# Attention feeding a Mish-gated MLP on one core: one attention output product moved ahead of the second group of exponentials, the MM2 portions dealt anew, and MM1's fourth block put in the second score tile

## The chip, the cores and the metric

The kernel runs on one core of one Trainium2 chip. Five engines work from queues of their own: TensorE (PE in the profile, with PEld for its weight loads), VectorE (DVE), ScalarE (ACT), GpSimd (POOL) and SyncE (SP, which here only issues DMAs). They wait for one another through semaphores. The metric is the device time of one execution in microseconds; the median of the runs is compared.

## What is computed

```python
# q, k, v: (8, 12, 448, 64); w_in: (768, 2048); w_out: (2048, 768)
scores = scale * np.matmul(q, k.transpose(0, 1, 3, 2))
m = np.max(scores, axis=-1, keepdims=True)
e = np.exp(scores - m)
attn = e / (np.sum(e, axis=-1, keepdims=True) + np.exp(-m) + 1e-09)
x = np.matmul(attn, v)                     # then heads side by side: (3584, 768)
h = x @ w_in
sp = np.where(h > 20.0, h, np.log1p(np.exp(np.minimum(h, 20.0))))
out = (h * np.tanh(sp)) @ w_out            # (3584, 768)
```

## The kernel before

Heads are worked in pairs: 8 batches of 6 pairs, 48 pairs in all, and three pairs make a unit, so there are 16 units of attention, two to a batch. The first units fill the machine. From unit 6 to unit 15, ten units, every unit has the same form, and the change is about these; the code calls them `grouped`.

**A unit's attention half** has twelve steps (`n`, 0 to 11). A step n is one score product on PE into one of three PSUM tiles sc0, sc1, sc2 (two banks each, 84, 85 and 86 in the built program's names), then the maximum of it on DVE (L369), then the exponentials on ACT (L387). Steps 0 to 8 fill both banks of a tile and take two exponentials; steps 9, 10 and 11 fill one bank and take one. Step n uses tile n mod 3, so the score of step n+3 may not start before the exponentials of step n have read their tile. I write score n, maximum n and exponentials n. In program order scores 0, 1 and 2 come at the very end of the unit before. Scores 3 and 4 are issued together after exponentials 1, scores 5 and 6 after exponentials 3, scores 7 and 8 after exponentials 5 (so that two products run at once on the halves of the PE array, L356 and L359), and scores 9, 10 and 11 one by one (L350).

**Between the steps** PE gets a filler: MM2, the second MLP product of an earlier group of rows (L616), in chunks of one matmul. A unit has three portions of 16 chunks with 384 columns and one portion of 16 chunks with 192 columns. A portion gathers in one of two further PSUM banks, mo0 and mo1 (87 and 88), and DVE copies it out (L601). The list `weight_paired` says how many chunks go in after which step, counted so that a wide chunk weighs 1, a narrow one a half, and a unit 56.

**The attention output** of a pair (`av_pair`, L497) is 8 matmuls, attention weights times v, for the three pairs of the unit before. Its operand eT is the normalised exponentials (DVE, L454), turned by a DMA that SP issues (L462) in the MM1 half of the unit before. All three products stand at step 8, behind the last filler: two in the free second banks of sc0 and sc1, copied by DVE (L517), the third in an mo bank, copied by ACT (L513) after exponentials 10. Score 11 follows them on PE.

**A unit's MLP half** is MM1: eight blocks of six matmuls of 448 columns (L556), each followed by Mish on ACT (L572) into `gT`. Exp and Mish lie in different activation tables, so ACT loads a table at both borders. Blocks 0 and 1 take the two mo banks, block 2 takes bank 0 of sc0, and blocks 3 to 7 take the mo banks in turn as Mish frees them. On DVE the MM1 half holds the denominators and the 21 normalisations.

The order on each engine is written out by hand: an engine runs its instructions in the order in which the loop makes them. Copies out of PSUM are put in a list `late`, which `flush_late` empties.

Of the kernel before, what the change touches and what calls it, by code (L numbers as in the profile page):

```python
# [15 lines left out]
UNIT_PAIRS = 3  # L16
# [3 lines left out]
def kernel(  # L20
# [17 lines left out]
    HP = H // 2  # L38
# [3 lines left out]
    UNITS_PER_B = HP // UNIT_PAIRS  # L42
    N_UNITS = B * UNITS_PER_B
    HU = 2 * UNIT_PAIRS
    FF_U = FF_T // UNITS_PER_B
# [7 lines left out]
    def pool(name, bufs, space=None):  # L53
# [16 lines left out]
    sc_tiles = [  # L70
        psum.tile([128, 2, 512], FP32, tag=f"sc{i}", name=f"sc{i}") for i in range(3)
    ]
# [43 lines left out]
    late, held, slow = deque(), deque(), deque()  # L116
    stores, defer = deque(), [False]

    def flush_late():
        while late:  # L120
            late.popleft()()
# [5 lines left out]
    def mo_take():  # L127

        if not mo_free:
            flush_late()  # L130
        return mo_free.popleft()
# [353 lines left out]
    def av_pair(p, half=None, hold=False, act=False):  # L485
        b, hp = p // HP, p % HP
        eT = att[p]["eT"]
        v_bf = casted[p]["v"]
        if b not in xT:
            xT[b] = xT_pool.tile([128, DM_T, S], BF16, tag="xT", name="xT")  # L490
        if half is not None:
            mms = av_beside.setdefault(last_step(half), [])
        av = mo_take() if half is None else free_half(half)
        for j in range(NT):
            for h in range(2):
                e_h = eT[0:SP_, j, h * S : (h + 1) * S]
                mm = nc.tensor.matmul(  # L497
                    av[h * 64 : (h + 1) * 64, 0:S],
                    lhsT=v_bf[:, h, j * D : (j + 1) * D],
                    rhs=e_h,  # L500
                    start=(j == 0), stop=(j == NT - 1),
                )
                if half is not None:
                    apart(mm, half_max[half])
                    mms.append(mm)

        def evac():
            to = xT[b][:, hp, :]
            if p == HP:
                apart(nc.scalar.copy(to, av[:, 0:S]), half_max[half])  # L510
                return
            if act:
                nc.scalar.copy(to, av[:, 0:S])  # L513
                mo_free.append(av)
                return
            if divided(p):
                read = nc.vector.tensor_copy(out=to, in_=av[:, 0:S])  # L517
            else:
                read = nc.vector.tensor_tensor(
                    out=to, in0=av[:, 0:S], in1=rb.pop(p), op=ALU.mult  # L520
                )
            if half in half_exp:
                apart(read, half_exp[half])
            elif half is not None:
                av_read[last_step(half)] = read
            if half is None:
                mo_free.append(av)

        if p in spread_copy:
            late.append(spread_copy.pop(p))  # L530
        (held if hold else slow if act or p == HP else late).append(evac)
        del att[p], casted[p], qkT[p]


# [1 line left out]

    def mm1_begin(b, ff, upto):

        bank = mm1_bank(ff)
        begun[b, ff] = (bank, upto)  # L540
        mm1(b, ff, bank, 0, upto)

# [4 lines left out]
            mm1(b, ff, bank, lo, DM_T)  # L547
            begun[b, ff] = (bank, DM_T)

    def mm1_bank(ff, ahead=2):  # L550
        at = ff % FF_U - 2
        return sc_tiles[0][:, at, :] if 0 <= at < ahead else mo_take()

    def mm1(b, ff, bank, lo, hi):
        for dm in range(lo, hi):
# [6 lines left out]

    def mm1_mish(b, ff):
        flush_late()
        at = ff % FF_U - 2
        spare = 0 <= at < (2 if b == 0 else 1)
        if (b, ff) in begun:
            h_ps, lo = begun.pop((b, ff))
        else:
            h_ps, lo = mm1_bank(ff, 2 if b == 0 else 1), 0  # L570
        mm1(b, ff, h_ps, lo, DM_T)
        nc.scalar.activation(out=gT[:, ff, b % 2 * S : b % 2 * S + S], in_=h_ps[:, 0:S], func=AF.Mish)  # L572
        if not spare:
            mo_free.append(h_ps)

    def store_rows(g, i, o_sb, cols, queue=None):
# [75 lines left out]

    weight = [5.2] + [1.0] * (steps - STEPS) + [0.4] * (STEPS - 1)
    PAIRED_FROM = first_mm2 + 2
    GROUP_AT, AV_AT_STEP = (1, 3, 5), 8
    Q_AT = (0, 6, 7)
    weight_paired = [21, 0, 12, 0, 12, 0, 5, 6, 0, 0, 0, 0]

    LEAD = UNIT_PAIRS + 1
    LOAD_AT = (0, 3, 6)  # L660
# [2 lines left out]
    BY_DMA_FROM = 2 * HP + 2 * UNIT_PAIRS  # L663
# [60 lines left out]
    for u in range(UNITS_PER_B, N_UNITS + 2 * UNITS_PER_B):  # L724
# [5 lines left out]
        p0 = u * UNIT_PAIRS  # L730
        grouped = attn and u >= PAIRED_FROM
# [7 lines left out]
        for n in range(steps):  # L739
            defer[0] = attn and u > first_mm2 and nxt < N_PAIRS  # L740
            pi, s = divmod(n, STEPS)
            p, idx = p0 + pi, p0 * STEPS + n
            late_tp = u == UNITS_PER_B and n == STEPS
            exps(idx)
            if u == UNITS_PER_B + 1 and n == 0:
                for j in range(2):
# [13 lines left out]
            while done < want:  # L760
                fn, w = filler.popleft()
                fn()
                done += w
            if grouped and n == AV_AT_STEP:
                for i in range(UNIT_PAIRS - 1):
                    av_pair(p0 + i - UNIT_PAIRS, half=p0 + i)
                flush_late()
                av_pair(p0 - 1, act=True)
            if not grouped or n + 1 not in GROUP_AT:
                scores_ahead(end)  # L770
            if n in LOAD_AT and u <= first_mm2:
                at = p0 + LOAD_AT.index(n)
# [23 lines left out]
            if (u, n) in MORE_LOADS:  # L796
                at = MORE_LOADS[u, n]
# [38 lines left out]
        b, w = (u - UNITS_PER_B) // UNITS_PER_B, u % UNITS_PER_B  # L836
# [3 lines left out]
        for f in range(FF_U):  # L840
# [22 lines left out]
            if f in (3, third) and p0 >= LATE_DIV:  # L863
                p = todo[1 + f // 5]
# [33 lines left out]
```

## Time and profile before

| what | value |
|---|---|
| median of 3 runs | 457.14 us (456.62 to 458.46) |
| the profiled execution, its own time | 459.73 us |
| its span, first to last instruction | 457.9 us |
| granted TensorE clock, mean over the span | 0.992 |
| grouped units 6 to 15 | 145.8 to 393.6 us of the span |
| instructions in the span | 8637 |

The page's first part gives each engine's busy time and the share of the span. A timeline row gives the start, the length, engine, line and operation, what is written and read, a count, and in brackets how long the engine stood idle and who released it. Matmuls overlap, so the length of one is longer than the distance from its start to the next one's start; rates are read from starts.

### The profile page before, as it was taken

Reading aid. Unit: us, or ns where it says so; the run is one execution under the profiler, and the core shown is the slowest. Engines: PE = TensorE matmul, PEld = TensorE weight load, DVE = VectorE, ACT = ScalarE, POOL = GpSimd, SP = SyncE. Lnnn points to the kernel's source line nnn. Section 1 sums busy time; section 2 is a strip of 40 time slices with the busy share of each in tenths; the row PEclk is TensorE's granted clock in tenths of the full one; section 3 lists DMA queues with packets and bytes.
Section 4 is the critical chain, followed back from the end, with each engine's and each line's share of the span. In section 5 each row is a group of like instructions: output and inputs, shape, how many; then the busy total and the mean of one; then the engine's idle time right before and its main releaser. Section 6 shows DMA issues by size and latency. Waiting matters only on the chain.

```text
span 457.9 us, 8637 instructions
## 1 busy us (share of the span) xinstructions
PE 436.2 (95%) x2991; PEld 232.1 (51%) x2991; DVE 327.3 (71%) x666; ACT 335.8 (73%) x884; POOL 138.6 (30%) x269
## 2 busy tenths in 40 slices
PE   7878699999999999999999999999999999999996
PEld 3334355445555545545454545554554555556565
DVE  5999678888797868778787878786878878311021
ACT  5999578989787969798887979796979788221300
POOL 4442638316054233232424242413233210100000
PEclk9999899999999999999999999999999999999999
DMA  8999999999999999999999999999999793920213
GB/s 233 260 209 162 246 227 212 264 235 207 242 238 273 237 279 241 250 230 283 236 257 236 259 253 229 266 214 273 229 245 252 205 243 106 246 65 2 69 36 103
DMA packets 232652, 97.93 MB, mean 214 GB/s; under 512 B 189344, under 2 KB 229152, under 8 KB 232608
## 3 DMA queue, kind: packets, MB, share of 16 engines
q1 hardware_dynamic: 225088, 91.07, 86.9%
q0 software_dynamic: 7488, 6.29, 9.3%
q8 instruction: 23, 0.38, 0.4%
q14 instruction: 21, 0.17, 0.1%
q10 hardware_dynamic: 32, 0.01, 0.0%
HBM read 45.61 MB, written 11.01 MB: 124 GB/s over the span
## 4 chain that ended last, share of the span: by engine, by line
PE 72%; ACT 10%; DVE 6%; issue 6%; DMA 3%; POOL 2%; DVEq 0%; ACTq 0%; POOLq 0%
PE mo L556 27%; PE mo L616 24%; ACT en L387 7%; PE sc L497 5%; PE sc L356 4%; PE sc L556 4%; DVE negm L369 4%; DMA eT<-en 3%; PE sc L350 2%; PE mo L497 2%; ACT L387 2%; POOL w_in_sb L177 1%; DVE o_sb L601 1%; PE sc L309 1%; DVE eT L477 1%
## 5 line engine op out<-in xcount | busy, mean ns | idle before, releaser
L387 ACT ACTIVATE en<-sc,negm 128x448 bf16<-128x448 f32 x336 | 208.9, 640 | 12.4 <-DVE negm L369 11.7
L369 DVE TENSOR_REDUCE negm<-sc 128x2 f32<-128x896 f32 x192 | 179.4, 970 | 48.5 <-PE sc L359 36.1
L616 PE MATMUL mo<-w_out_sb,gT 128*128 128x384 bf16 (+1 forms) x1040 | 159.1, 304 | 0.0
L556 PE MATMUL mo<-xT,w_in_sb 128*128 128x448 bf16 x660 | 131.7, 353 | 0.9 <-DVE xT L517 0.3
L616 PEld LDWEIGHTS <-gT 128*128 128x128 bf16 x1040 | 93.9, 98 | 60.8 <-issue 13.9
L556 PEld LDWEIGHTS <-w_in_sb 128*128 128x128 bf16 x768 | 74.3, 98 | 70.9 <-issue 5.1
L572 ACT ACTIVATE gT<-mo 128x448 bf16<-128x448 f32 x110 | 58.3, 544 | 67.9 <-PE mo L556 67.7
L387 ACT ACTIVATION_READ_ACCUMULATOR en<-sc,negm 128x1 f32 x336 | 71.0, 211 | 0.0
L454 DVE TENSOR_SCALAR en<-en,rden 128x448 bf16<-128x448 bf16 x280 | 70.6, 331 | 0.6
L601 DVE COPY o_sb<-mo 128x192 f32<-128x192 f32 (+1 forms) x65 | 32.4, 498 | 50.2 <-PE mo L616 49.0
L273 POOL TENSOR_SCALAR qd<-qT_all 64x448 bf16<-64x448 bf16 x60 | 33.6, 560 | 89.2 <-DMA qT_all<-q_cast 49.3
L356 PE MATMUL sc<-kT_all,qd 64*128 64x448 bf16 x132 | 42.0, 363 | 2.7 <-ACT en L387 1.3
L359 PE MATMUL sc<-kT_all,qd 64*128 64x448 bf16 x132 | 42.5, 367 | 0.0
L782 POOL COPY marks<-en 1x2 bf16<-1x2 bf16 x12 | 2.1, 174 | 105.6 <-DVE en L454 105.6
L194 POOL CAST q_cast<-q_f 112x512 bf16<-112x512 f32 x47 | 28.9, 614 | 5.8 <-DMA q_f<-in_q_dram 5.8
L497 PEld LDWEIGHTS <-v_bf 112*64 112x64 bf16 x384 | 19.8, 110 | 20.8 <-issue 10.4
L497 PE MATMUL sc<-eT,v_bf 112*64 112x448 bf16 x256 | 29.2, 364 | 0.4 <-DMA eT<-en 0.4
L194 POOL CAST k_cast<-k_f 112x512 bf16<-112x512 f32 x47 | 28.8, 612 | 1.5 <-DMA k_f<-in_k_dram 1.4
L194 POOL CAST v_bf<-v_f 112x512 bf16<-112x512 f32 x48 | 28.2, 607 | 2.4 <-DMA v_f<-in_v_dram 2.4
L556 PE MATMUL sc<-xT,w_in_sb 128*128 128x448 bf16 x108 | 23.2, 353 | 0.0
L356 PEld LDWEIGHTS <-qd 64*128 64x128 bf16 x132 | 9.1, 95 | 26.7 <-issue 17.9
L350 PE MATMUL sc<-kT_all,qd 128*128 128x448 bf16 x60 | 19.2, 353 | 1.3 <-ACT en L387 1.1
(64 smaller groups left out, 267.8 us busy)
## 6 DMA issues: line engine op xcount, KB each, us to landing
k_f<-in_k_dram SPq DMA_DIRECT2D x48, 224.0 KB, 5.2
q_f<-in_q_dram SPq DMA_DIRECT2D x48, 224.0 KB, 5.3
v_f<-in_v_dram SPq DMA_DIRECT2D x48, 224.0 KB, 5.8
w_in_sb<-in_moe_w_in_dram POOLq DMA_DIRECT2D x12, 256.0 KB, 7.3
w_out_sb<-in_moe_w_out_dram POOLq DMA_DIRECT2D x8, 384.0 KB, 12.2
out_dram<-o_sb SPq DMA_DIRECT2D x7, 336.0 KB, 3.3
out_dram<-o_sb SPq DMA_DIRECT2D x8, 288.0 KB, 3.5
out_dram<-o_sb SPq DMA_DIRECT2D x8, 240.0 KB, 3.0
```

The source lines that it names most:

```text
L194: nc.gpsimd.tensor_copy(out=to[nm], in_=src)
L273: q_reads.append(by.tensor_scalar(out=qd[rows, h * S : (h + 1) * S], in0=q_ps[rows, 0:S], scalar1=SCALE, scalar2=1.0, op0=ALU.mult, op1=AL ...
L356: nc.tensor.matmul(sc[:, 0, 0:S], lhsT=qT[0:64, qa : qa + 128], rhs=kA, start=True, stop=True)
L359: nc.tensor.matmul(sc[:, 1, 0:S], lhsT=qT[64:128, qb : qb + 128], rhs=kB, start=True, stop=True)
L369: half_max[p] = nc.vector.tensor_reduce(out=negm, in_=sc[:, 0 : len(cols), 0:S], axis=AX.X, op=ALU.max, negate=True)
L387: e = nc.scalar.activation(out=st["en"][:, :, c, 0:SP_], in_=sc[:, bk, 0:S].rearrange("q (j c) -> q j c", j=NT), func=AF.Exp, bias=st["neg ...
L454: nc.vector.tensor_scalar(out=en[:, :, i, 0:SP_], in0=en[:, :, i, 0:SP_], scalar1=st["rden"][:, i : i + 1], scalar2=None, op0=ALU.mult,)
L497: mm = nc.tensor.matmul(av[h * 64 : (h + 1) * 64, 0:S], lhsT=v_bf[:, h, j * D : (j + 1) * D], rhs=e_h, start=(j == 0), stop=(j == NT - 1),)
L556: nc.tensor.matmul(bank[:, 0:S], lhsT=w_in_sb[:, dm, ff * 128 : (ff + 1) * 128], rhs=xT[b][:, dm, :], start=(dm == 0), stop=(dm == DM_T - 1),)
L572: nc.scalar.activation(out=gT[:, ff, b % 2 * S : b % 2 * S + S], in_=h_ps[:, 0:S], func=AF.Mish)
L601: nc.vector.tensor_copy(out=o_sb[:, cols], in_=st["o"][:, 0:n_cols])
L616: nc.tensor.matmul(st["o"][:, 0:n_cols], lhsT=gT[:, ff, i * 128 : (i + 1) * 128], rhs=w_out_sb[:, ff, cols], start=(ff == 0), stop=(ff == ...
```

## The change

In a grouped unit the output product of the first pair of the unit before moves from step 8 to step 3: it follows the fillers of step 2 and stands ahead of scores 5 and 6. It gathers in an mo bank and ACT copies it ahead of exponentials 4. The other two stay at step 8 and both go to the second banks of sc0 and sc1. The portions of MM2 are dealt 21, 6, 14, 5, 10 instead of 21, 12, 12, 5, 6. In units 5 to 17 the fourth block of MM1 takes bank 0 of sc1 instead of an mo bank.

```diff
-        (held if hold else slow if act or p == HP else late).append(evac)
+        (held if hold else slow if p == HP else late).append(evac)
...
-        bank = mm1_bank(ff)
+        bank = mm1_bank(b, ff)
...
-    def mm1_bank(ff, ahead=2):
-        at = ff % FF_U - 2
-        return sc_tiles[0][:, at, :] if 0 <= at < ahead else mo_take()
+    def mm1_spare(b, ff):
+
+        u, at = (b + 1) * UNITS_PER_B + ff // FF_U, ff % FF_U - 2
+        if at == 0 or (at == 1 and b == 0):
+            return sc_tiles[0][:, at, :]
+        if at == 1 and (u + 1) * UNIT_PAIRS >= BY_DMA_FROM:
+            return sc_tiles[1][:, 0, :]
+
+    def mm1_bank(b, ff):
+        spare = mm1_spare(b, ff)
+        return mo_take() if spare is None else spare
...
-        at = ff % FF_U - 2
-        spare = 0 <= at < (2 if b == 0 else 1)
...
-            h_ps, lo = mm1_bank(ff, 2 if b == 0 else 1), 0
+            h_ps, lo = mm1_bank(b, ff), 0
...
-        if not spare:
+        if mm1_spare(b, ff) is None:
             mo_free.append(h_ps)
...
-    GROUP_AT, AV_AT_STEP = (1, 3, 5), 8
+    GROUP_AT, AV_AT_GROUP, AV_AT_STEP = (1, 3, 5), 3, 8
...
-    weight_paired = [21, 0, 12, 0, 12, 0, 5, 6, 0, 0, 0, 0]
+    weight_paired = [21, 0, 6, 0, 14, 0, 5, 10, 0, 0, 0, 0]
...
+            if grouped and n == AV_AT_GROUP + 1:
+                flush_late()
             exps(idx)
...
+            if grouped and n == AV_AT_GROUP:
+                av_pair(p0 - UNIT_PAIRS, act=True)
             if grouped and n == AV_AT_STEP:
-                for i in range(UNIT_PAIRS - 1):
-                    av_pair(p0 + i - UNIT_PAIRS, half=p0 + i)
+                for i in range(1, UNIT_PAIRS):
+                    av_pair(p0 + i - UNIT_PAIRS, half=p0 + i - 1)
                 flush_late()
-                av_pair(p0 - 1, act=True)
```

What moves in a grouped unit shows on ACT and DVE. First ACT, from the table load at the start of the exponentials to the next unit's Mish; `en` are the exponentials, `xT` the transposed attention output that MM1 reads, `x2` the two banks of a step. Before:

```order
L387 ACTIVATE en_108,sums<-sc_84,negm 128x4x112 x2
L387 ACTIVATE en_108,sums<-sc_85,negm 128x4x112 x2
L387 ACTIVATE en_108,sums<-sc_86,negm 128x4x112 x2
L387 ACTIVATE en_104,sums<-sc_84,negm 128x4x112 x2
L387 ACTIVATE en_104,sums<-sc_85,negm 128x4x112 x2
L387 ACTIVATE en_104,sums<-sc_86,negm 128x4x112 x2
L387 ACTIVATE en_107,sums<-sc_84,negm 128x4x112
L387 ACTIVATE en_108,sums<-sc_85,negm 128x4x112
L513 CAST xT<-mo_88 128x448
L385 ACTIVATE expm<-negm 128x21
L387 ACTIVATE en_104,sums<-sc_86,negm 128x4x112
```

The same stretch, exponentials 3 to 11, in the change:

```order
L387 ACTIVATE en_108,sums<-sc_84,negm 128x4x112 x2
L513 CAST xT<-mo_87 128x448
L387 ACTIVATE en_108,sums<-sc_85,negm 128x4x112 x2
L387 ACTIVATE en_108,sums<-sc_86,negm 128x4x112 x2
L387 ACTIVATE en_104,sums<-sc_84,negm 128x4x112 x2
L387 ACTIVATE en_104,sums<-sc_85,negm 128x4x112 x2
L387 ACTIVATE en_104,sums<-sc_86,negm 128x4x112 x2
L387 ACTIVATE en_107,sums<-sc_84,negm 128x4x112
L387 ACTIVATE en_108,sums<-sc_85,negm 128x4x112
L385 ACTIVATE expm<-negm 128x21
L387 ACTIVATE en_104,sums<-sc_86,negm 128x4x112
```

The copy of an attention output has moved from behind exponentials 10 to between exponentials 3 and 4. Next the eight Mish of the MM1 half on ACT, whose second names are the banks of MM1's blocks 0 to 7. Before:

```order
L572 ACTIVATE gT<-mo_87 128x448
L572 ACTIVATE gT<-mo_88 128x448
L572 ACTIVATE gT<-sc_84 128x448
L572 ACTIVATE gT<-mo_87 128x448
L572 ACTIVATE gT<-mo_88 128x448
L572 ACTIVATE gT<-mo_87 128x448
L572 ACTIVATE gT<-mo_88 128x448
L572 ACTIVATE gT<-mo_87 128x448
```

In the change:

```order
L578 ACTIVATE gT<-mo_87 128x448
L578 ACTIVATE gT<-mo_88 128x448
L578 ACTIVATE gT<-sc_84 128x448
L578 ACTIVATE gT<-sc_85 128x448
L578 ACTIVATE gT<-mo_87 128x448
L578 ACTIVATE gT<-mo_88 128x448
L578 ACTIVATE gT<-mo_87 128x448
L578 ACTIVATE gT<-mo_88 128x448
```

Block 3 no longer reuses block 0's bank; block 4 now does. Last DVE, from maximum 5 to maximum 11 of a unit; `negm` are the maxima and `o_sb` the MM2 rows copied out. Before:

```order
L601 COPY o_sb<-mo_87 128x384
L369 TENSOR_REDUCE negm<-sc_86 128x2
L369 TENSOR_REDUCE negm<-sc_84 128x2
L369 TENSOR_REDUCE negm<-sc_85 128x2
L369 TENSOR_REDUCE negm<-sc_86 128x2
L601 COPY o_sb<-mo_88 128x384
L369 TENSOR_REDUCE negm<-sc_84 128x1
L369 TENSOR_REDUCE negm<-sc_85 128x1
L601 COPY o_sb<-mo_87 128x192
L517 CAST xT<-sc_84 128x448
L517 CAST xT<-sc_85 128x448
L369 TENSOR_REDUCE negm<-sc_86 128x1
```

In the change:

```order
L369 TENSOR_REDUCE negm<-sc_86 128x2
L369 TENSOR_REDUCE negm<-sc_84 128x2
L607 COPY o_sb<-mo_88 128x384
L369 TENSOR_REDUCE negm<-sc_85 128x2
L369 TENSOR_REDUCE negm<-sc_86 128x2
L369 TENSOR_REDUCE negm<-sc_84 128x1
L607 COPY o_sb<-mo_87 128x384
L369 TENSOR_REDUCE negm<-sc_85 128x1
L607 COPY o_sb<-mo_88 128x192
L517 CAST xT<-sc_84 128x448
L517 CAST xT<-sc_85 128x448
L369 TENSOR_REDUCE negm<-sc_86 128x1
```

The copies of the second and third portion stand later, behind maximum 6 and maximum 9. The two casts of attention outputs stand at the same place, ahead of maximum 11, but are now those of the unit's second and third pair. POOL and SP have the same instructions in the same order in both kernels.

## The prediction

> **What bounds the kernel now.** I read the page first, then the grouped units apart, then one unit's chain and its engines' timelines.
>
> ```profile
> span 457.9 us, 8637 instructions
> PE 436.2 (95%) x2991; PEld 232.1 (51%) x2991; DVE 327.3 (71%) x666; ACT 335.8 (73%) x884; POOL 138.6 (30%) x269
> ...
> PE 72%; ACT 10%; DVE 6%; issue 6%; DMA 3%; POOL 2%; DVEq 0%; ACTq 0%; POOLq 0%
> ```
>
> PE is busy 95% of the span and holds 72% of the chain of waits. The table by stretches, one grouped unit to a row (length, then busy time of PE, PEld, DVE, ACT, POOL):
>
> ```profile
> 145.79:170.56 24.77, 24.66 (x158) 12.70 (x158) 19.76 (x41) 20.81 (x54) 8.07 (x16) 1.00 1.08 260
> 220.11:244.88 24.77, 24.57 (x158) 12.71 (x158) 19.75 (x41) 20.75 (x54) 8.50 (x17) 1.00 1.11 238
> 368.74:393.58 24.84, 24.63 (x159) 12.90 (x159) 19.75 (x41) 20.75 (x54) 1.42 (x4) 1.00 0.73 181
> ```
>
> Each of the ten lasts 24.77 us (the last 24.84), at a granted clock of 1.00. So the question is what one unit gains, times ten. A busy PE may still stand: a matmul's length overlaps the next, so I look at distances between starts, in the unit that begins at 220.11.
>
> ```profile
> 220.78 3.59 PE L616 MATMUL mo<-w_out_sb,gT 128*128 128x384 bf16 x21
> 224.30 0.36 PE L356 MATMUL sc<-kT_all,qd 64*128 64x448 bf16 x1
> 224.75 0.35 PE L356 MATMUL sc<-kT_all,qd 64*128 64x448 bf16 x1
> 225.05 2.12 PE L616 MATMUL mo<-w_out_sb,gT 128*128 128x384 bf16 x12
> 227.11 0.36 PE L356 MATMUL sc<-kT_all,qd 64*128 64x448 bf16 x1
> 227.31 0.35 PE L356 MATMUL sc<-kT_all,qd 64*128 64x448 bf16 x1
> 227.59 2.12 PE L616 MATMUL mo<-w_out_sb,gT 128*128 128x384 bf16 x12
> 229.65 0.36 PE L356 MATMUL sc<-kT_all,qd 64*128 64x448 bf16 x1
> 230.10 0.35 PE L356 MATMUL sc<-kT_all,qd 64*128 64x448 bf16 x1
> ...
> 231.33 0.35 PE L350 MATMUL sc<-kT_all,qd 128*128 128x448 bf16 x1
> 231.52 1.15 PE L616 MATMUL mo<-w_out_sb,gT 128*128 128x192 bf16 x12
> 232.64 0.35 PE L350 MATMUL sc<-kT_all,qd 128*128 128x448 bf16 x1
> 232.92 1.70 PE L497 MATMUL sc<-eT,v_bf 112*64 112x448 bf16 x16
> 234.46 0.92 PE L497 MATMUL mo<-eT,v_bf 112*64 112x448 bf16 x8
> 235.31 0.36 PE L350 MATMUL sc<-kT_all,qd 128*128 128x448 bf16 x1
> 235.51 2.43 PE L556 MATMUL mo<-xT,w_in_sb 128*128 128x448 bf16 x12
> 237.78 1.30 PE L556 MATMUL sc<-xT,w_in_sb 128*128 128x448 bf16 x6
> 239.11 5.84 PE L556 MATMUL mo<-xT,w_in_sb 128*128 128x448 bf16 x30
> 244.88 0.36 PE L356 MATMUL sc<-kT_all,qd 64*128 64x448 bf16 x1
> ```
>
> These are scores 3 to 11 (first halves where two run at once), the fillers, the three outputs and MM1. Score 6 follows score 5 after 0.20; scores 4 and 8 follow their partners after 0.45, so PE stands 0.25 there. MM1 runs at (237.78 - 235.51) / 12 = 0.189 a matmul, so block 2 would be over at 238.92; block 3 starts at 239.11, **0.19 late**. ACT's timeline tells why:
>
> ```profile
> 226.53 0.62 ACT L387 ACTIVATE en<-sc,negm 128x448 bf16<-128x448 f32 x1
> 227.14 0.63 ACT L387 ACTIVATE en<-sc,negm 128x448 bf16<-128x448 f32 x1
> 228.71 0.63 ACT L387 ACTIVATE en<-sc,negm 128x448 bf16<-128x448 f32 x1 [0.23 <-DVE negm L369]
> 229.33 0.62 ACT L387 ACTIVATE en<-sc,negm 128x448 bf16<-128x448 f32 x1
> 231.88 0.62 ACT L387 ACTIVATE en<-sc,negm 128x448 bf16<-128x448 f32 x1
> 235.48 0.53 ACT L513 CAST xT<-mo 128x448 bf16<-128x448 f32 x1 [0.43 <-PE mo L497]
> 236.37 0.22 ACT L385 ACTIVATE expm<-negm 128x21 f32<-128x21 f32 x1 [0.36 <-DVE negm L369]
> 238.52 0.98 ACT L572 ACTIVATE gT<-mo 128x448 bf16<-128x448 f32 x2
> 239.38 0.55 ACT L572 ACTIVATE gT<-sc 128x448 bf16<-128x448 f32 x1
> ```
>
> The second half of exponentials 5 starts at 229.33 and score 8 at 230.10, 0.77 later: the tile is free then. Exponentials 3 (second half 226.53) release score 6 at 227.31, 0.78 later, so score 6 is just on time; exponentials 7 (231.88) release score 10 at 232.64, 0.76 later. PE therefore goes at ACT's pace at scores 4, 6, 8 and 10. Mish 0 starts at 238.52 and frees block 0's bank for block 3 at 239.11, 0.59 later.
>
> **The change part by part.** Nothing is added or removed: the same matmuls, copies and DMAs. The numbers below are for this unit.
>
> *MM1's fourth block.* Bank 0 of sc1 was last read by exponentials 10, before the copy at 235.48. Block 3 starts at once: **0.19 saved**. The next to reuse block 0's bank is block 4, 6 x 0.189 = 1.13 later. Is Mish 0 late for it? DVE now has to cast the second of the two last outputs ahead of maximum 11:
>
> ```profile
> 230.12 2.09 DVE L369 TENSOR_REDUCE negm<-sc 128x2 f32<-128x896 f32 x2 [0.45 <-ACT en L387]
> ...
> 233.92 1.37 DVE L517 CAST xT<-sc 128x448 bf16<-128x448 f32 x2
> 235.72 0.62 DVE L369 TENSOR_REDUCE negm<-sc 128x1 f32<-128x448 f32 x1 [0.42 <-PE sc L350]
> ...
> 245.29 1.09 DVE L369 TENSOR_REDUCE negm<-sc 128x2 f32<-128x896 f32 x1 [2.25 <-PE sc L359]
> ```
>
> The first cast starts 233.92, 1.00 after its output's first matmul (232.92), and the two take 1.37, so 0.69 each. The second output's first matmul will lie 0.85 ahead of score 11 (234.46 to 235.31, as the last one's did), so its cast runs from 0.15 to 0.84 after score 11, where maximum 11 began at 0.41 (235.72). Maximum 11, the last exponentials and Mish 0 come **0.43 later** against score 11. Mish 0 freed its bank 3.80 after score 11 (239.11); now 4.23. Block 4 arrives 0.20 + 24 x 0.189 = 4.74 after score 11. The 0.5 between hides the delay; without it, up to 0.4 a unit would be paid. The normalisations on DVE slide by the same 0.4 and by the shorter unit; the idle 2.25 ahead of the next maximum 0 covers that.
>
> *The first output at step 3.* From first chunk to next score 21 chunks take 3.52 (220.78 to 224.30) and 12 take 2.06 (225.05 to 227.11): (3.52 - 2.06) / 9 = 0.1625 a chunk, and 0.11 for the change of product. Six from 225.05 bring the output to 226.13 (before: 12, and scores at 227.11). Its 8 matmuls and the step to a score take 235.31 - 234.46 = 0.85: score 5 at 226.98. Score 6 still waits for exponentials 3 until 227.31. By PE alone score 6 would go at 227.18, so 0.13 of waiting is left there, which would also hide a switch that costs up to 0.13 more than these rows. The moved work costs nothing here; the cover is exponentials 3.
>
> ACT's copy can start 1.02 after the output's first matmul (234.46 to 235.48): 227.15, just when exponentials 3 leave ACT (226.53 + 0.61 = 227.14). It lengthens ACT's queue by 0.43 (two Mish from 238.52, the third at 239.38) to 0.53 (its own length). Behind it are exponentials 4 (before 227.14), now 227.58 to 227.68, and 5 (before 228.71, after an idle 0.23), now 1.22 later at 228.80 to 228.90. Of the half microsecond, 0.1 to 0.2 gets through. Score 8 then is free at 230.19 to 230.29 (before 230.10). PE meanwhile does 14 chunks from 227.59, 0.11 + 14 x 0.1625 = 2.39, so scores 7 and 8 would start at 229.98 and 230.18: PE hardly stands at all there.
>
> *The end of the attention half.* Exponentials 6 follow with the same delay and free score 9 at 231.42 to 231.52 (before 231.33; by PE alone 231.35). Then 0.19, two wide chunks (0.33) and 16 narrow ones at half a wide chunk's 0.1625 (1.30; the row of 12 bounds one at (232.64 - 231.52) / 12 = 0.093): score 10 at 233.24 to 233.34, or 0.1 later if a score needs that behind a narrow chunk, which no row shows unhindered. It no longer waits for ACT: score 7 at 229.98, its maximum 0.47 later (229.65 to 230.12), exponentials 7 another 1.1 later (two maxima take 2.09), second half 0.63, tile free 0.78 later: 232.96. Then 0.28 and two outputs, 2.39 less 0.77 (232.92 to 235.31, and half of 232.92 to 234.46): score 11 at 235.14 to 235.34, at the early end I think, against 235.31 before. **-0.17 to +0.03**, taken as -0.10.
>
> *Sum.* -0.19 - 0.10 = -0.29 a unit, bounds -0.36 and -0.16; ten units, **-2.9 us** (-3.6 to -1.6). Units 5, 16 and 17 also get the new bank; their blocks 3 had no wait that I could find, so nothing. The tail behind unit 15 starts earlier by the same amount. Span 457.9 becomes 455.0, and the profiled execution's own time, 459.73, would fall alike; the median of the runs, 457.14, lies 2.6 below that time, and I carry the difference over to it: **454.2**, -0.64%.
>
> **The rivals.**
>
> *Slower: the first output waits for its DMA.* The first of the three products stood at 232.92 and now stands at 226.13, 6.8 us earlier in the unit, and its eT is turned late in the unit before. Of the ten units' first transposes the slowest was:
>
> ```profile
> L462 SPq DMA_TRANSPOSE eT<-en x1: 5937/5937/5937, 314.2 to 314.2; - x1
> DMA to landing us min/median/max: 9.5/9.5/9.5
> ```
>
> It was issued 314.2 and landed at 323.7. The next unit, which starts at 319.2 (four units of 24.77 after 220.11), would want it 6.0 in, at 325.2; with the transposes 0.4 later and the unit's start 0.3 earlier 0.8 is left. Waits begin at a landing 10.3 us after issue, the gain is gone at 10.6, and each further tenth costs 1 us over ten units, for ACT's copy and all exponentials stand behind it. If the tighter unit pushed loads into every transpose and it took 11.0: 457.1 + 4 = 461. For it: the transposes share SP's queue with nine loads and up to six stores a unit. Against: no landing of the ten is that late.
>
> *ACT's copy sets the pace.* If the exponentials behind it come later by the full 0.53 instead of 0.1 to 0.2, score 9 comes at 231.33 + 0.53 = 231.86 and score 11 at 235.58, 0.27 later than before; against Mish's 0.19 that is +0.08 a unit, 457.9, no change to be told. For it: scores 6 and 8 are at ACT's pace already. Against: the idle 0.23 ahead of exponentials 5.
>
> *Only the wait for Mish goes.* The output's move breaks even: -0.19 a unit, 455.2. That is what comes out if the two borders of the moved product that no row shows, a wide chunk to an output and an output to paired scores, cost 0.1 more each than the 0.08 that a shown one does (an output 0.28 after a score where MM1 follows one after 0.20), past the 0.13 that hides them, or if a score starts late behind a narrow chunk.
>
> [...]
>
> *More than forecast.* If score 4's 0.25 shrinks too, as the border shifts: -0.5 a unit, 452.2. No row speaks for it.
>
> That the change doesn't do what it says is ruled out by the order of ACT and DVE shown above.
>
> **How the numbers follow.** Forecast 0.55; only Mish's wait 0.2; ACT's pace 0.1; DMA 0.08; more 0.07. The likeliest one's own range is 453.4 to 455.0. To hold 8 in 10 I take 453.0 to 456.6, which covers the bounds of the sum and the case of Mish's wait alone, and leaves out the DMA case, the gain of 0.5 and most of ACT's pace. Half a per cent, 2.3 us, is about what a measurement of this kernel can tell from no change. Below 454.85: 0.55 + 0.07 = 0.62. Within: 0.2 + 0.1 = 0.30. Above 459.4: the DMA case, 0.08.
>
> **What would show it.** Right: units of about 24.48; no gap between blocks 2 and 3 of MM1; score 6 at 7.2 after the unit's start as before, score 8 at 10.1 to 10.2, score 11 near 15.1; ACT's copy directly behind exponentials 3; Mish 0 some 0.4 later against score 11 and no wait at block 4. Wrong: the output at step 3 released by a DMA, PE standing more than 0.2 ahead of score 9 or 10, or a stop at block 4.

## The result, and the profile after

| what | before | changed |
|---|---|---|
| median (runs) | 457.73 us (18 runs, 454.61 to 460.46) | 455.56 us (18 runs, 452.72 to 462.45) |
| ratio | | 0.9954, 95% interval 0.9932 to 0.9975 |
| profiled span | 457.9 us | 454.6 us |
| start of unit 6, first score | 145.79 us | 144.41 us |
| units 6 to 15 together | 247.63 us | 245.67 us |

The change is 2.2 us faster, 0.46%, with the interval from 0.25% to 0.68%. One run of the changed kernel, 462.45 us, was clearly slower than its others and is left out of the ratio. The two spans differ by 3.3 us, but 1.4 of these lie ahead of unit 6, where the two programs do nearly the same: over all profiled executions of this study unit 6 starts anywhere from 141.8 to 147.0. The ten grouped units gave 1.96 us. I count them to the first MM2 chunk behind the last unit's MM1, which before starts at 393.42; by this the last unit before lasts 24.68 us, and the 24.84 of the prediction's row ends 0.16 later. I therefore judge every kernel below by its units first, and by medians second.

The table by stretches of the changed kernel, one grouped unit to a row (length, then busy time of PE, PEld, DVE, ACT, POOL with their counts, the granted clock, the DMA share and GB/s), shows the 1st, 4th, 8th and 10th of the ten:

```profile
144.41:168.96 24.55, 24.52 (x158) 12.60 (x158) 19.78 (x41) 20.73 (x54) 7.84 (x16) 1.00 1.08 254
217.85:242.34 24.49, 24.40 (x158) 12.61 (x159) 20.00 (x41) 20.63 (x54) 8.45 (x17) 1.00 1.14 242
315.71:341.24 25.53, 24.46 (x158) 12.52 (x157) 20.74 (x41) 20.70 (x54) 8.82 (x17) 1.00 1.16 249
365.69:390.08 24.39, 24.30 (x158) 12.72 (x158) 19.77 (x41) 20.63 (x54) 1.67 (x4) 1.00 0.75 181
```

Nine units last 24.39 to 24.55, 0.2 to 0.3 shorter than before. The eighth lasts 25.53, and its busy PE time is no longer than the others': for about 1 us PE stands. PE's timeline of the fifth unit, which starts at 242.34 (from the fillers behind score 4 on; of paired scores one half is shown), answers to the rows shown of before:

```profile
247.22 1.15 PE L622 MATMUL mo<-w_out_sb,gT 128*128 128x384 bf16 x6
248.30 0.95 PE L497 MATMUL mo<-eT,v_bf 112*64 112x448 bf16 x8
249.18 0.36 PE L356 MATMUL sc<-kT_all,qd 64*128 64x448 bf16 x1
...
249.53 0.35 PE L356 MATMUL sc<-kT_all,qd 64*128 64x448 bf16 x1
...
249.82 2.45 PE L622 MATMUL mo<-w_out_sb,gT 128*128 128x384 bf16 x14
252.21 0.36 PE L356 MATMUL sc<-kT_all,qd 64*128 64x448 bf16 x1
...
252.43 0.35 PE L356 MATMUL sc<-kT_all,qd 64*128 64x448 bf16 x1
...
253.66 0.35 PE L350 MATMUL sc<-kT_all,qd 128*128 128x448 bf16 x1
253.85 1.81 PE L622 MATMUL mo<-w_out_sb,gT 128*128 128x384 bf16 x18
255.49 0.35 PE L350 MATMUL sc<-kT_all,qd 128*128 128x448 bf16 x1
255.77 1.70 PE L497 MATMUL sc<-eT,v_bf 112*64 112x448 bf16 x16
257.41 0.36 PE L350 MATMUL sc<-kT_all,qd 128*128 128x448 bf16 x1
257.61 2.43 PE L564 MATMUL mo<-xT,w_in_sb 128*128 128x448 bf16 x12
259.88 2.43 PE L564 MATMUL sc<-xT,w_in_sb 128*128 128x448 bf16 x12
262.15 4.70 PE L564 MATMUL mo<-xT,w_in_sb 128*128 128x448 bf16 x24
```

Blocks 2 and 3 of MM1 now run as one row of 12 and block 4 follows after 2.27, which is 12 x 0.189: no stop at either. Against the unit's start, score 6 comes at 7.19, score 8 at 10.09, score 9 at 11.32, score 10 at 13.15 and score 11 at 15.07 (before: 7.20, 9.99, 11.22, 12.53, 15.20). The output's eight matmuls and the step to the paired score 5 take 249.18 - 248.30 = 0.88, and the six chunks ahead of it 1.08. ACT's timeline of the same unit has its new copy:

```profile
248.76 0.62 ACT L387 ACTIVATE en<-sc,negm 128x448 bf16<-128x448 f32 x1
249.37 0.53 ACT L513 CAST xT<-mo 128x448 bf16<-128x448 f32 x1
249.78 0.65 ACT L387 ACTIVATE en<-sc,negm 128x448 bf16<-128x448 f32 x1
...
251.01 0.66 ACT L387 ACTIVATE en<-sc,negm 128x448 bf16<-128x448 f32 x1
...
260.86 0.98 ACT L578 ACTIVATE gT<-mo 128x448 bf16<-128x448 f32 x2
```

The copy stands directly behind exponentials 3 and holds the queue for 0.41. Exponentials 4 start at 7.44 after the unit's start (before 7.03), exponentials 5 at 8.67 (before 8.60): of 0.41 only 0.07 is left, as the idle 0.23 took most of it. Mish 0 (260.86) starts 3.45 after score 11, where it stood at 3.21 before. DVE's timeline has the reason:

```profile
256.76 1.38 DVE L517 CAST xT<-sc 128x448 bf16<-128x448 f32 x2
258.06 0.61 DVE L369 TENSOR_REDUCE negm<-sc 128x1 f32<-128x448 f32 x1
```

Maximum 11 waits for the second cast and starts 0.65 after score 11 (before 0.41).

In the eighth unit PE's timeline reads:

```profile
320.65 1.15 PE L622 MATMUL mo<-w_out_sb,gT 128*128 128x384 bf16 x6
322.78 0.95 PE L497 MATMUL mo<-eT,v_bf 112*64 112x448 bf16 x8 [0.98 <-DMA eT<-en]
```

The output at step 3 waits 0.98 for its eT. SP's timeline shows why that is late (issue is the start of SP's instruction for a DMA, landing the arrival of the data):

```profile
304.02 3.26 SPq L590 DMA_DIRECT2D out_dram<-o_sb  x6
...
310.31 0.46 SPq L143 DMA_DIRECT2D q_f<-in_q_dram  x1
310.81 2.05 SPq L143 DMA_DIRECT2D v_f<-in_v_dram  x3
313.35 14.19 SPq L462 DMA_TRANSPOSE eT<-en  x3
```

SP went from six stores through nine loads with hardly a pause and reached the transposes at 313.35, 22.1 after the first score of the unit (291.27); before, all ten units' first transposes went out at 19.5 to 19.8. The first one landed 9.4 us after its issue, no later than the slowest one before (9.5). Its operand had long been ready: the unit's seventh normalisation, the last one that this transpose needs, ended on DVE at 311.16, 2.19 before the issue, while in the other nine units only 0.06 to 0.07 lie between the two. So in this unit SP's queue was late. Before the change SP came to the same transposes just in time:

```profile
312.15 1.47 SPq L143 DMA_DIRECT2D v_f<-in_v_dram  x3
314.16 5.94 SPq L462 DMA_TRANSPOSE eT<-en  x1
```

This is 0.55 behind its last load and 0.25 behind the seventh normalisation.

### The profile page after: what moved, and what is told of

Its sections match the earlier page's. It is cut to its first block, busy times and chain, and to the rows that moved or that the text cites. A ratio compares the mean times of both kernels' runs of the same rounds, so it can differ in the third digit from the quotient of the medians.

```text
span 454.6 us, 8630 instructions
## 1 busy us (share of the span) xinstructions
PE 436.0 (96%) x2991; PEld 232.5 (51%) x2991; DVE 330.3 (73%) x666; ACT 334.7 (74%) x884; POOL 139.1 (31%) x269
## 4 chain that ended last, share of the span: by engine, by line
PE 71%; ACT 10%; DMA 7%; DVE 7%; SPq 2%; issue 2%; DVEq 0%; ACTq 0%
PE mo L622 25%; PE mo L564 21%; ACT en L387 7%; PE sc L564 7%; DMA eT<-en 6%; PE sc L356 5%; PE sc L497 5%; DVE negm L369 4%; PE mo L497 3%; PE sc L350 2%; DMA v_f<-in_v_dram 1%; ACT L387 1%; DVE eT L477 1%; PE sc L309 1%; SPq L143 1%
## 5 line engine op out<-in xcount | busy, mean ns | idle before, releaser
L564 PE MATMUL mo<-xT,w_in_sb 128*128 128x448 bf16 x582 | 116.5, 352 | 0.6 <-DVE xT L517 0.3
L578 ACT ACTIVATE gT<-mo 128x448 bf16<-128x448 f32 x97 | 51.3, 545 | 60.5 <-PE mo L564 60.3
L454 DVE TENSOR_SCALAR en<-en,rden 128x448 bf16<-128x448 bf16 x280 | 72.6, 337 | 0.6
L387 ACT ACTIVATION_READ_ACCUMULATOR en<-sc,negm 128x1 f32 x336 | 72.1, 215 | 0.0
L564 PE MATMUL sc<-xT,w_in_sb 128*128 128x448 bf16 x186 | 38.0, 353 | 0.0
L578 ACT ACTIVATE gT<-sc 128x448 bf16<-128x448 f32 x31 | 16.8, 550 | 4.7 <-PE sc L564 3.6
```

The source lines that it names most:

```text
L387: e = nc.scalar.activation(out=st["en"][:, :, c, 0:SP_], in_=sc[:, bk, 0:S].rearrange("q (j c) -> q j c", j=NT), func=AF.Exp, bias=st["neg ...
L454: nc.vector.tensor_scalar(out=en[:, :, i, 0:SP_], in0=en[:, :, i, 0:SP_], scalar1=st["rden"][:, i : i + 1], scalar2=None, op0=ALU.mult,)
L564: nc.tensor.matmul(bank[:, 0:S], lhsT=w_in_sb[:, dm, ff * 128 : (ff + 1) * 128], rhs=xT[b][:, dm, :], start=(dm == 0), stop=(dm == DM_T - 1),)
```

## The experiments

Each kernel is the changed one with the edit shown, unless the text says otherwise. "Units" is the length of the ten grouped units together.

**The new bank alone.** The kernel before, with `mm1_spare` of the change; the outputs and portions stay as they were.

```diff
+        if at == 1 and (u + 1) * UNIT_PAIRS >= BY_DMA_FROM:
+            return sc_tiles[1][:, 0, :]
```

> The change's new bank for MM1's fourth block alone; the outputs and the portions stand as before. My theory: block 3 follows block 2 after 0.189 and the ten grouped units are 24.58 us each, 0.19 under before, no output waits for its transposes, 1.9 us less in all (-0.4%). The rival, that the later reuse of block 0's bank by block 4 takes the wait over: a stop of about 0.2 ahead of block 4 and units of 24.77.

Measured: 455.33 us, ratio 0.9964 (0.9932 to 0.9997). Units 245.73; nine of 24.58 and the last 24.49. No output waits, though the seventh unit's first transpose took 10.0 us to land. The bank is worth 0.19 a unit. By time the bank alone is not told from the whole change (0.9964 and 0.9954, with intervals that overlap).

**The output and the portions alone.** Block 3 goes back to an mo bank.

```diff
-        if at == 1 and (u + 1) * UNIT_PAIRS >= BY_DMA_FROM:
-            return sc_tiles[1][:, 0, :]
```

> The moved output and the new portions alone; block 3 of MM1 goes back to an mo bank. My theory: the two parts don't add up. Mish 0 comes about 0.25 later against score 11 than before, since two casts stand ahead of maximum 11, so block 3 stops 0.44 instead of 0.19; score 11 is 0.1 earlier; units of 24.9 us, 1 to 2 us more than before in all. The rival, that the parts are independent: a stop of 0.19, units of 24.65, 1 us less than before.

Measured: 458.5 us, ratio 1.003 (1.0001 to 1.0059). Units 248.96, 24.9 each. Here is PE's timeline from score 11 of the unit that starts at 243.06, and below it ACT's Mish:

```profile
258.13 0.36 PE L350 MATMUL sc<-kT_all,qd 128*128 128x448 bf16 x1
...
260.60 1.30 PE L562 MATMUL sc<-xT,w_in_sb 128*128 128x448 bf16 x6
262.18 4.51 PE L562 MATMUL mo<-xT,w_in_sb 128*128 128x448 bf16 x23 [0.28 <-ACT gT L576]
```

```profile
261.58 0.98 ACT L576 ACTIVATE gT<-mo 128x448 bf16<-128x448 f32 x2
```

Block 3 starts 1.58 after block 2, where six matmuls take 1.13: PE loses 0.44 (the bracket counts from the modelled end). Mish 0 starts 3.45 after score 11, 0.24 later than before. So the moved output is a loss without the new bank: it brings the unit's scores forward by some 0.12 and sends Mish 0 back by 0.24. The parts don't add: -0.19 and +0.13 a unit apart, -0.31 together.

**Output one group later.** It stands at step 5, ahead of scores 7 and 8, and the portions are shifted to fit.

```diff
-    GROUP_AT, AV_AT_GROUP, AV_AT_STEP = (1, 3, 5), 3, 8
+    GROUP_AT, AV_AT_GROUP, AV_AT_STEP = (1, 3, 5), 5, 8
...
-    weight_paired = [21, 0, 6, 0, 14, 0, 5, 10, 0, 0, 0, 0]
+    weight_paired = [21, 0, 12, 0, 8, 0, 5, 10, 0, 0, 0, 0]
```

> The changed kernel with the moved output two steps later: at step 5, ahead of scores 7 and 8, its copy ahead of exponentials 6, the portions dealt 21, 12, 8, 5, 10. My theory: the place matters because ACT stood 0.23 idle ahead of exponentials 5 and nowhere else; here the whole copy goes into ACT's queue, exponentials 6 come at 10.3 and score 9 at 11.7 instead of 11.3, and a unit is 24.8 us, so the gain of the bank is given back and the time is that of the kernel before within 1 us. No output waits for transposes. The rival, that any step ahead of the last one does: units of 24.45 and 3 us less than before.

Measured: 458.2 us, ratio 1.0019 (0.9978 to 1.006). Units 248.4, 24.79 to 24.89 each. The first transposes of all ten units go out at 20.0 to 20.1 and nothing waits for them, but the chunks between score 8 and score 9 are too few to hide the copy on ACT:

```profile
253.22 0.99 PE L622 MATMUL mo<-w_out_sb,gT 128*128 128x384 bf16 x5
254.67 0.35 PE L350 MATMUL sc<-kT_all,qd 128*128 128x448 bf16 x1 [0.46 <-ACT en L387]
```

**ACT's copy made twice.**

```diff
                 nc.scalar.copy(to, av[:, 0:S])
+                nc.scalar.copy(to, av[:, 0:S])
```

> The changed kernel with the copy of the moved output made twice on ACT, to price what lies in ACT's queue there. My theory: the idle time ahead of exponentials 5 is used up, so the second copy gets through in full: 0.43 a unit, scores 8 and 9 later by that, units of 24.85 to 24.9. The rival, that ACT's queue is hidden behind PE there: units stay 24.45.

Measured: 460.64 us in one run. Units 249.9, 25.00 each, 0.54 more than the changed kernel undisturbed (24.46), where 0.43 was expected. The table of what PE waited for (total, times, longest) puts it on score 8:

```profile
PE sc L356 <- ACT en L387: 5.5, 12, 0.7
```

The first copy cost 0.1 at score 8; the second costs its whole length. The cover at step 3 is used up by one copy.

**The third pair at step 3.** The output whose eT is turned last stands at step 3, the other two at step 8.

```diff
-                av_pair(p0 - UNIT_PAIRS, act=True)
+                av_pair(p0 - 1, act=True)
...
-                for i in range(1, UNIT_PAIRS):
-                    av_pair(p0 + i - UNIT_PAIRS, half=p0 + i - 1)
+                for i in range(UNIT_PAIRS - 1):
+                    av_pair(p0 + i - UNIT_PAIRS, half=p0 + i)
```

> The changed kernel with the third pair's output at step 3 instead of the first's, the first and second at step 8. The third pair's transposes are issued some 7 to 8 us after the first's. My theory: each unit waits at step 3 for the landing and pays it in full, since the next normalisations move with the unit's end: 1.5 to 2.5 us a unit, units of 26.0 to 26.9, 15 to 25 us in all. The rival, that such a wait is made up within the unit, PE being ahead of ACT behind it: less than 0.5 a unit.

Measured: 487.99 us in one run. Units of 26.0 to 29.9; PE waits in all ten:

```profile
PE mo L497 <- DMA eT<-en: 22.7, 10, 3.9
```

The loss, 275.4 - 244.6 = 31 us of units, is larger than the 22.7 of waiting and than the 15 to 25 expected: behind a wait of 2.40 the granted clock was 0.50 (last section), and its mean over this run was 0.965, against 0.985 in the first profile of the changed kernel. It shows that a transpose that is late for step 3 is paid in full, and that the third pair's is not early enough; the second pair's was not tried.

**Stores from another queue.** My first theory for the wait in the eighth unit: SP is busy with six stores. Here POOL issues the stores.

```diff
-            (queue if queue is not None and n < SP_ else nc.sync).dma_start(
+            (nc.gpsimd if pool else queue if queue is not None and n < SP_ else nc.sync).dma_start(
...
-                stores.append(lambda: store_rows(g, i, o_sb, slice(0, d_model)))
+                stores.append(lambda: store_rows(g, i, o_sb, slice(0, d_model), pool=True))
```

> The changed kernel, with the stores of finished rows issued from POOL's queue instead of SP's. The changed kernel's profile has one unit of 25.5 us whose moved output waits 1.05 us for its transposes, issued 2.3 us late by SP behind six stores. My theory, that SP's queue is what was late: with the stores gone from it, every unit's first transposes are issued within 0.5 us of the same place in the unit, no moved output waits, all ten units 24.44 to 24.49, about 1 us less than the changed kernel. The rival, that the DMA engines are full and the queue only shows it: the transposes of that unit land as late as before and the wait of about 1 us stays.

Measured: 464.06 us, ratio 1.0104 (1.0068 to 1.014); the profiled execution took 468.42 us, so its rows show more than the median has. SP's lateness is gone: in all ten units the first transpose is issued 0.06 to 0.07 after the seventh normalisation, and no output at step 3 waits. But PE now waits at step 8, whose banks are those of `sc`:

```profile
PE sc L497 <- DMA eT<-en: 5.2, 4, 2.9
```

The units are 24.4 to 24.8 but for two of 26.14 and 30.44, in which step 8 waits 1.51 and 2.88 for the third pair's transposes; these landed 11.7 and 12.6 us after their issue. In the second of the two the first transposes go out 24.7 after the first score, since the normalisations too are late there. The group of the kT transposes (duration in ns, minimum, median, maximum), first here, then in the changed kernel:

```profile
L205 SPq DMA_TRANSPOSE kT_all<-k_cast x9: 1277/1462/5417, 153.8 to 359.2; - x9
```

```profile
L205 SPq DMA_TRANSPOSE kT_all<-k_cast x9: 1348/1358/1368, 151.2 to 350.6; - x9
```

With SP's queue rid of the stores, stores and transposes run side by side (in one unit POOL's six stores go out from 200.5 to 203.1 and land 4.1 to 8.5 later, and the kT transpose that SP issues at 204.5 takes 4.73 to issue), and a transpose that took 1.36 us to issue takes up to 5.4. So the theory was right that SP's queue was late, and wrong that nothing else would be: the time that it promised did not come. The rival, that the DMA engines are full, fits the longer transposes, and the page's row of slices has the engines busy at nine tenths or more in most slices up to the tail; but it has them so before the change as well. That the transposes took longer for want of DMA engines is not shown by this run, since the stores changed in kind as well: the page counts POOL's as `software_dynamic` (16.9 MB instead of 6.3), and their medians from issue to landing, size by size, are 4.8 to 6.5 us instead of 2.7 to 3.9.

**The changed kernel again, three times.**

> The changed kernel once more, for a second profile. If the wait for the transposes belongs to the unit that follows six stores, it is seen again in the unit at about 316 us, by 0.5 to 1.5 us, and nine units are 24.44 to 24.49. If it is a chance of that execution, it is somewhere else or nowhere.

> The changed kernel a third time, with more rounds. Without a wait for transposes its units sum to 244.6 us, 3.1 under before; with the wait seen once, to 245.7, 2.0 under. If the wait is rare, the median is 0.6 to 0.7% under before; if it comes in most executions, 0.4%.

> The changed kernel once more, a fourth profile: three so far show the wait for eT in the same unit twice (25.53 and 27.91 us) and once not at all. If it is the backlog behind the six-store unit, a wait appears only in the unit that follows that one or not at all, and the other nine are 24.4 to 24.6; if any late DMA does it, it may appear in any unit.

Measured: 454.63 us (one run); 455.54 us (12 runs), ratio 0.9948 (0.991 to 0.9987); 456.64 us (one run). The table (its last three rows are kernels told of below) gives, for the seventh unit, when the first transpose went out and how long it took to land, then what the eighth unit's output did:

| profile | issued after the unit's first score | landed after | wait for eT | eighth unit | units |
|---|---|---|---|---|---|
| before | 19.73 | 9.5 | none (step 8) | 24.77 | 247.63 |
| changed, first | 22.08 | 9.4 | 0.98 | 25.53 | 245.67 |
| changed, second | 19.65 | 9.0 | none | 24.47 | 244.55 |
| changed, third | 22.38 | 10.2 | 2.06 | 27.91 | 247.99 |
| changed, fourth | 22.28 | 9.7 | 1.50 | 26.06 | 246.30 |
| at most two rows' stores a unit | 20.51 | 10.2 | 0.2 | 24.78 | 245.36 |
| third row's stores left out | 19.65 | 8.3 | none | 24.47 | 244.54 |
| eighth unit as before | 21.73 | 9.6 | none (step 8) | 24.58 | 244.65 |

Three of four show the wait, always in this one unit, which follows a unit with six stores; the fourth unit follows one too and never waits. Landing times hardly differ; the issue does, by up to 2.7. Behind the seventh normalisation it comes 2.19, 1.98 and 1.63 late in the three profiles with a wait and 0.06 in the one without. What takes more of SP's time where it is late are the three eT transposes of the sixth unit; here they are before, in the changed kernel's first profile and in its second:

```profile
289.20 11.38 SPq L462 DMA_TRANSPOSE eT<-en  x3
```

```profile
287.46 13.56 SPq L462 DMA_TRANSPOSE eT<-en  x3
```

```profile
286.17 10.93 SPq L462 DMA_TRANSPOSE eT<-en  x3
```

In the third and fourth they take 14.34 and 14.59; in these two and the first they also start 0.6 later in their unit than in the second. The instructions of the six stores behind them take 2.8 to 3.0 of SP's time in all four profiles of the changed kernel, and 3.4 before, so it is not the stores' own time that differs.

Undisturbed, the change takes 3.1 us from the ten units; the waits take 0 to 3.4 back, 1.6 in the mean of the four. The mean of the four sums, 246.13, is thus no lower than the 245.73 of the one profile of the bank alone: what the moved output gains undisturbed, the waits took back.

**At most two rows' stores in a unit.** A third row's stores are held until the next unit.

```diff
-    def flush_stores():
-        while stores:
+    def flush_stores(most=99):
+        while stores and most:
             stores.popleft()()
+            most -= 1
...
-                flush_stores()
+                flush_stores(2)
```

> The changed kernel, but the stores of at most two finished MM2 rows (four stores) go out in a unit; where a unit has finished three, the third row's two are held until the next unit's turn. My theory: every fourth unit issues six stores on SP between the transposes and the loads, SP has no spare time left there, and in a unit that is 0.3 shorter the next first transpose then goes out up to 2.6 us late (22.1 to 22.4 us after its unit's first score instead of 19.7 to 20.1), which the output at step 3 waits for now and then. With at most four stores every first transpose of units 6 to 15 goes out within 0.5 of 19.7 to 20.1, no output waits for a DMA, the units are 24.4 to 24.6 each and 244.6 in sum. Price that could eat it: a copy of MM2 rows on DVE that waits for a held store to free its buffer. Rival: the wait has nothing to do with the number of stores and stays where it was (one unit of 25.5 to 27.9, sum 245.7 to 248).

Measured: 453.67 us (6 runs), ratio 0.99 (0.9859 to 0.994), the lowest median of the study. But the units don't bear my reason out. First transposes went out at 21.6 to 22.1 in four of the ten units instead of two or none, and two units were lengthened by waits for eT, one at step 8 and one at step 3:

```profile
264.11:289.11 25.00, 24.58 (x158) 12.69 (x158) 21.48 (x43) 20.61 (x54) 8.66 (x16) 1.00 1.16 244
...
313.55:338.32 24.77, 24.45 (x158) 12.52 (x158) 20.67 (x41) 20.68 (x54) 8.60 (x16) 1.00 1.10 253
```

Spreading the stores spread the lateness. The sum, 245.36, is 2.3 below before; the profiled execution also began unit 6 at 141.77, among the earliest, and that part is the same program. Its interval overlaps that of the change, so it is not shown to be better.

**The third row's stores left out.** This kernel leaves part of the output unwritten and serves as a test alone.

```diff
+                while len(stores) > 2:
+                    stores.pop()
                 flush_stores()
```

> The changed kernel without the stores of the third finished MM2 row in the units that have finished three: these rows of the output are not written, all else is computed. My theory (six stores are what makes SP late): all first transposes of units 6 to 15 within 0.5 of 19.7 to 20.1 us after their unit's first score, no wait for eT, units 244.6 in sum. Rival (anything else on the DMA queues): a stop of 0.2 or more at the output of step 3 in at least one of the ten units, sum 245.7 or above.

Measured: 454.51 us in one run. All ten first transposes go out at 19.65 to 19.91, no output waits, and the ten units take 244.54. The group of all eT transposes in these units (duration in ns, then time to landing), here first and then in the changed kernel:

```profile
L462 SPq DMA_TRANSPOSE eT<-en x33: 3408/3643/5320, 138.2 to 390.9; - x33
...
DMA to landing us min/median/max: 5.0/5.3/8.3
```

```profile
L462 SPq DMA_TRANSPOSE eT<-en x33: 3534/3733/6351, 139.0 to 392.7; - x33
...
DMA to landing us min/median/max: 5.0/5.6/9.6
```

The slowest transpose goes out in 5.3 instead of 6.4 and lands after 8.3 instead of 9.6. Taken with the kernel that only spreads the stores: how much SP issues and the engines move over these units decides whether the transposes are late, and not that six stores stand in one unit. Which of the two it is, these kernels do not tell, since a store left out takes both away.

**The eighth unit as before.** In this one unit all three outputs stay at step 8, with the portions of before; the other nine are the changed kernel's.

```diff
+    OLD_AT, weight_old = 13, [21, 0, 12, 0, 12, 0, 5, 6, 0, 0, 0, 0]
...
-            if grouped and n == AV_AT_GROUP:
+            if grouped and u != OLD_AT and n == AV_AT_GROUP:
                 av_pair(p0 - UNIT_PAIRS, act=True)
...
+                if u == OLD_AT:
+                    av_pair(p0 - 1, act=True, wait=True)
```

> The changed kernel, but in one of the ten units, the eighth, in which three of four profiles of the changed kernel show the wait for eT (0.8 to 3.5 us), all three outputs stay at step 8 with the portions of before (block 3's new bank stays). My theory: the DMA queue has no time to spare over several units and the late first transposes pile up until this unit; an output that is wanted some 6 us later there waits for nothing, so the eighth unit takes about 24.6 whatever the transposes do, the others 24.4 to 24.6 as in the undisturbed profile of the changed kernel, 244.7 in sum, 2.9 us below the kernel before: ratio about 0.994, and better than the changed kernel by the 1 us or so that the wait costs it on average. Rival: the delay moves on and another unit's output waits instead, sum 245.5 or more, no better than the changed kernel.

Measured: 454.18 us (12 runs), ratio 0.9946 (0.9912 to 0.998). The seventh and eighth units:

```profile
289.89:314.32 24.43, 24.40 (x158) 12.61 (x159) 20.07 (x41) 20.59 (x54) 8.09 (x16) 1.00 1.10 257
314.32:338.90 24.58, 24.41 (x158) 12.71 (x158) 21.24 (x41) 20.75 (x54) 8.53 (x16) 1.00 1.10 250
```

The seventh unit's first transpose was late again (21.73, landing 6.9 after the eighth unit's start, where step 3 would have wanted it at 6.0), and nobody waited. Units 244.65, 3.0 below before, as expected. By time it is not told from the changed kernel; by the units of its one profile it has the gain without a wait. The lateness did move on in part, as the rival has it: the eighth unit's first transpose went out at 21.03 and landed 5.5 after the ninth unit's start, 0.4 ahead of its step 3. Of the versions tried it is the one I would keep.

## Why the prediction was right, and where it was off

The prediction was 454.2 in 453.0 to 456.6; measured 455.56. Of its three bands the time fell in the middle one, which had 0.30, and not in the one below 454.85, which had 0.62. By its own steps:

- **MM1's fourth block, -0.19: right.** The bank alone makes the unit 24.58 instead of 24.77, and no gap is left between blocks 2 and 3.
- **Mish 0 later by 0.43, hidden by the new bank: the size was off, the rest right.** It is 0.24 later. The term that was mis-sized is the second cast: I let it start 0.15 after score 11, but it follows the first one directly, and maximum 11 starts 0.65 after score 11 instead of 0.84. Block 4 hides it, and the kernel without the bank pays 0.25 more than before.
- **The output at step 3, -0.10: right** (24.58 to 24.46, -0.12). Score 8 came at 10.09 (predicted 10.1 to 10.2), score 11 at 15.07 (15.1), and exponentials 5 0.07 later (0.1 to 0.2).
- **The sum, -2.9: right for an undisturbed execution**, -3.08 in the second profile of the changed kernel and -3.0 with the eighth unit as before.
- **The rival of the DMA: underrated, and its mechanism misplaced.** I fixed the transpose's issue at its place in the unit and asked for a landing of more than 10.3 us; the landings stayed at 9.0 to 10.2. The issue itself slipped by 2.3 to 2.7, behind DMA work on SP that does not shrink with the unit; with less of it, the issue is punctual again (19.65 to 19.91 with the third row's stores left out). In the kernel before, the gap on SP between the last load and the next transpose was already 0.55 behind the six stores of the seventh unit (2.62 in the unit ahead of it), and the prediction left this out. The price is not 4 us in each execution but 0 to 3.4 in one unit, 1.6 in the mean: -3.1 + 1.6 = -1.5, beside the -2.2 of the medians (-1.1 to -3.1 by the interval). Of the 1.36 by which the time lies above the forecast, 0.6 is the kernel before, whose median came out as 457.73 and not 457.14, and 0.7 a smaller gain, for which the waits are enough. That the time stayed in the range is in part luck: nothing in the prediction bounded these waits.
- **ACT's copy sets the pace: not so**, but there is no cover left, as the doubled copy shows.
- **Only the wait for Mish goes: not so.** The row of the output to the paired score, 0.88 against 0.85 to a single one, and the 1.08 of six chunks, 0.105 more than 6 x 0.1625, price the two new borders at about 0.1 each. The measured 455.56 is nearer to the 455.2 of Mish's wait alone than to 454.2, but by chance: that would make units of 24.58, and undisturbed ones last 24.46.

What stays open: why the sixth unit's transposes hold SP for 10.9 us in one of four executions of the changed kernel and for 13.6 to 14.6 in the others. SP's queue is what was late in the seventh unit. That its transposes grow when the DMA engines have more to do fits the kT transposes beside POOL's stores, but is not shown for these; the same bytes in other pieces were not tried.

## What to carry to other kernels

When a consumer is moved earlier, its producer has to be followed back to the queue that issues it, and that queue's spare time read unit by unit, in the unit with the most work on it; a landing time alone does not tell when the issue will slip. A shorter loop takes its gain out of the slack of everything that does not shrink with it. Two edits in one change can depend on each other: here one alone gains 0.19 a unit, the other alone loses 0.13, and both gain 0.31 where no transpose is late.

## What the hardware showed that I had not expected

Here a wait of PE cost more than its length. In the third profile of the changed kernel PE stood for 2.06 us, and the unit was 3.4 us longer than in the undisturbed profile (27.91 against 24.47). PE's timeline and the stretches behind the wait (PEclk is the third figure from the end):

```profile
321.23 1.35 PE L497 MATMUL mo<-eT,v_bf 112*64 112x448 bf16 x8 [2.06 <-DMA eT<-en]
```

```profile
321.20:321.60 0.40, 0.37 (x4) 0.25 (x6) 0.00 (x0) 0.00 (x0) 0.00 (x0) 1.00 1.27 289
321.63:325.04 3.41, 3.41 (x16) 1.12 (x13) 1.87 (x2) 2.37 (x8) 0.00 (x0) 0.50 1.27 289
325.04:327.00 1.96, 1.96 (x14) 0.85 (x12) 0.70 (x2) 1.86 (x7) 0.00 (x0) 1.00 1.14 260
```

The granted clock fell from 1.00 to 0.50 0.4 after PE had resumed, for 3.41 us, and the output took 1.35 instead of 0.95. After the waits of 0.98 and 1.50 the clock stayed at 1.00. In the kernel with the third pair at step 3 it was 0.50 from 156 to 158 us of the span, behind a wait of 2.40, and the output there took 1.18.
